# Keys and queries of a linear-attention block, computed for paired token tiles as seven block products instead of eight

## The chip, the cores and the metric

The kernel runs on one core of one Trainium2 chip. The metric is device time in microseconds (us) of one execution. Runs of the kernel before took 1123.71, 1124.23 and 1126.42 us; their median, 1124.23, is the time to compare with.

A core has a matrix engine, TensorE (PE in the profile; PEld is its weight load), a vector engine, VectorE (DVE), ScalarE (ACT), GpSimd (POOL), and a queue on SyncE (SP) that issues all transfers (DMAs) here. They share an on-chip memory (SBUF); TensorE writes to a small accumulator memory (PSUM) of eight banks, which the other engines empty.

## The reference

For 2,048 tokens of 576 features in fp32:

```python
xn = layernorm(x)
q, k, v = split(xn @ wqkv)              # 32 heads of 18
phi = lambda t: where(t > 0, t + 1, exp(t)) + 1e-6
kv = einsum("hsd,hse->hde", phi(k), v); z = phi(k).sum(over tokens)
s = (phi(q) @ kv) / (phi(q) . z + 1e-6) @ wo
g = silu(gelu(xn @ w1 + b1) @ w2 + b2)  # 4608 hidden
out = x + s * g
```

## The kernel before, in words

**Arithmetic.** TensorE multiplies in a rounded fp32 format (fp32r). So each fp32 operand is split into a high part (a cast, on ACT) and a low part (operand minus high part, on DVE or POOL), and a product of 128 rows of the contraction takes three matmuls: high x high, high x low, low x high. The 576 features are four blocks of 128 and a rest of 64, whose high and low parts lie in one tile of 128 rows. So the projection of one token tile of 128 to 576 columns is 14 steps, each in two halves of 288 columns: 28 matmuls of 128x288 (`project`, L219).

**Stage 1 (0 to 153 us).** For each of 16 token tiles: layernorm statistics (`layernorm`, DVE L168 to L180, a power on POOL L173), the normalized tile xn (ACT, L191), five transposes on TensorE (L196), the split of the transposed tile (ACT L204, DVE L205 and L206), K and V projections (L219), phi of K (L226 to L229), and the state kv, a sum over tokens kept in two banks (`state`, L256). Beside this the 27 sums of blocks of w2 that the last stage needs are made: subtraction on POOL (L288), cast on ACT (L296), low part on DVE (L301), a store. The weights are split at the start (`split_w`, L243 and L244).

**Stage 2 (153 to 298 us).** kv is folded with wo into one matrix (`fold_wo`, L518 to L525, right after the first two queries). For each tile: Q projection (`query`, L219), phi, the denominators (POOL L546, DVE L550 to L554, POOL L555), five transposes (`transpose_p`, L574), and 28 matmuls with the folded matrix (`attend`, L592). Beside this, `XSums` makes sums and differences of blocks of x (L337 to L341) in long operations for each half of the tokens.

**Stage 3 (298 to 1122 us).** The two layers of the feed-forward part, for two halves of 1,024 tokens in nine chunks of hidden features each. Each layer multiplies 2 x 2 blocks with seven block products instead of eight (a Strassen scheme with operands summed ahead): `Up` (L819, moving operand 128x512) and the products of the second layer (L950). At the half switch x's operands of the second half are loaded from device memory (`load_x_part`, L1115, seven DMAs of 8.1 MB together); the last chunk of the second half is done in plain products (`down_plain`, L1074 and L1087).

**What sets the order.** In stages 1 and 2 every instruction stands in its engine's queue in the order of the program text (`in_order`): an instruction that waits holds up all behind it on its engine. All DMAs stand in one queue. PSUM has three tiles of two banks, used in turn for transposes, K, V, Q and `attend`, and two single banks, for the state and for `fold_wo`.

## Time and profile before

| what | before |
|---|---|
| median of three runs | 1124.23 us |
| span of the profiled execution | 1122.4 us |
| mean granted TensorE clock | 0.995 of full speed |
| PE busy, share of the span | 1108.1 us, 99% |
| DVE / ACT / POOL busy | 811.9 / 456.8 / 443.0 us |
| moved by DMA | 246.7 MB, mean 220 GB/s |

The profile is of one execution; its span runs from the first to the last instruction, and the time of an execution is about 1.8 us above it. A window row gives, for a stretch of time, each engine's busy time with its number of instructions, the granted TensorE clock, the share of time that the DMA engines were busy, and GB/s. A timeline row gives start and duration of neighbouring like instructions, and in brackets the idle time of the engine before them and what ended it. A row of instruction groups gives the line, the engine, the operation, output<-inputs, shapes, the count, then busy time, the mean of one in ns, and the idle time before.

### The profile page before, as it was taken

What the parts mean: (1) busy time and instruction counts of PE and PEld (TensorE: products, weight loads), DVE (VectorE), ACT (ScalarE), POOL (GpSimd) and SP (SyncE); (2) the same over time, 40 slices, a digit from 0 to 9 for tenths busy, and PEclk for the clock granted to TensorE, in tenths of its full rate; (3) what the DMA queues carried; (4) which work ended last, traced back from release to release, by engine and by line L of the source; (5) the groups of instructions that cost most, each with busy time, mean ns of one, the idle gap of its engine ahead of it and who ended that gap; (6) DMA issues with size and microseconds to landing.
All of it is one profiled execution on the core that took longest, in us unless ns stands there. A gap on an engine that the chain in (4) does not pass through costs nothing.

```text
span 1122.4 us, 18619 instructions
## 1 busy us (share of the span) xinstructions
PE 1108.1 (99%) x7008; PEld 1026.8 (91%) x7008; DVE 811.9 (72%) x1185; ACT 456.8 (41%) x801; POOL 443.0 (39%) x368
## 2 busy tenths in 40 slices
...
GB/s 295 193 335 301 222 124 41 33 172 160 228 224 342 170 241 301 160 290 206 205 340 172 262 244 389 368 254 258 221 208 212 214 204 211 231 197 222 84 170 88
DMA packets 83367, 246.71 MB, mean 220 GB/s; under 512 B 9229, under 2 KB 19981, under 8 KB 79695
## 3 DMA queue, kind: packets, MB, share of 16 engines
...
q8 instruction: 55, 0.90, 0.3%
...
## 4 chain that ended last, share of the span: by engine, by line
PE 95%; DVE 3%; DMA 0%; POOL 0%; ACT 0%; issue 0%; SPq 0%; DVEq 0%; ACTq 0%; POOLq 0%
PE pm L950 34%; PE e L819 12%; PE a L819 10%; PE zy L819 10%; PE pv L219 5%; PE pk L219 5%; PE b L819 4%; PE ps_s L592 4%; PE pq L219 4%; PE pd L1074 2%; PE ps_kva L256 1%; PE pt L196 1%; DVE xt L337 1%; PE ps_kw L518 1%; PE ptp L574 0%; DMA w<-wqkv 0%
## 5 line engine op out<-in xcount | busy, mean ns | idle before, releaser
L957 DVE TENSOR_TENSOR macc<-pm,macc 128x576 f32<-128x576 f32 x218 | 164.2, 753 | 56.9 <-PE pm L950 56.3
L616 ACT CAST h_h<-g 128x512 fp32r<-128x512 f32 x204 | 120.9, 621 | 139.8 <-PE pm L950 138.7
L619 DVE TENSOR_TENSOR h_l<-g,h_h 128x512 fp32r<-128x512 f32 x204 | 172.3, 844 | 0.0
L918 POOL TENSOR_TENSOR mid<-g 128x512 f32<-128x512 f32 x34 | 44.1, 1296 | 187.7 <-ACT g L827 187.7
L827 ACT ACTIVATE g<-b,b1c 128x512 f32<-128x512 f32 x36 | 24.8, 688 | 121.8 <-DVE b L845 121.7
L836 ACT COPY mid<-a 128x512 f32<-128x512 f32 x36 | 21.1, 585 | 109.3 <-PE a L819 109.3
L819 PE MATMUL a<-h0r,wa 128*128 128x512 f32 x180 | 58.6, 390 | 0.0
L819 PE MATMUL a<-xh,wa 128*128 128x512 f32 x180 | 58.5, 390 | 0.0
L839 DVE TENSOR_TENSOR mid<-b,mid 128x512 f32<-128x512 f32 x36 | 24.8, 689 | 46.5 <-PE b L819 35.4
L915 POOL TENSOR_TENSOR g<-g 128x512 f32<-128x512 f32 x34 | 52.4, 1542 | 13.1 <-DVE h_l L619 11.8
L912 POOL TENSOR_TENSOR g<-g 128x512 f32<-128x512 f32 x34 | 49.5, 1456 | 17.9 <-DVE h_l L619 16.6
L1044 POOL TENSOR_TENSOR fin1l<-fin1h,fin1l 128x288 f32<-128x288 f32 x8 | 6.4, 805 | 121.4 <-DMA fin1l<-s_dram 45.1
L819 PE MATMUL zy<-xh,w 128*128 128x512 f32 x144 | 50.2, 389 | 0.0
L819 PE MATMUL zy<-h1r,w 128*128 128x512 f32 x144 | 50.2, 389 | 0.0
L641 POOL TENSOR_TENSOR w1t<-w1raw 128x256 f32<-128x256 f32 x18 | 17.6, 977 | 81.4 <-DVE w L619 81.4
L909 POOL TENSOR_TENSOR g<-g 128x512 f32<-128x512 f32 x34 | 47.7, 1402 | 2.7
L852 DVE TENSOR_TENSOR e<-e,mid 128x512 f32<-128x512 f32 x36 | 25.1, 697 | 27.1 <-PE e L819 27.0
L555 POOL TENSOR_TENSOR pbuf<-phiq,den 128x576 f32<-128x576 f32 x16 | 20.9, 1305 | 57.8 <-DVE den L554 52.9
L827 ACT ACTIVATE g<-e,b1c 128x512 f32<-128x512 f32 x36 | 24.8, 689 | 43.0 <-DVE e L852 43.0
L288 POOL TENSOR_TENSOR w2r<-w2r 128x576 f32<-128x576 f32 x27 | 41.1, 1528 | 0.7
L819 PEld LDWEIGHTS a<-xh,wa 128*128 128x128 f32 x180 | 33.8, 188 | 6.8
L819 PEld LDWEIGHTS a<-h0r,wa 128*128 128x128 f32 x180 | 33.8, 188 | 6.8
...
## 6 DMA issues: line engine op xcount, KB each, us to landing
...
```

The lines of the kernel that those rows point to most:

```text
L219: nc.tensor.matmul(ps[:, h, :HD], st, w[:, k, h * HD : (h + 1) * HD], start=(i == 0), stop=(i == len(seq) - 1),)
L592: nc.tensor.matmul(ps[:, h, :HD], st[:, k, :], w[:, k, h * HD : (h + 1) * HD], start=(i == 0), stop=(i == len(seq) - 1),)
L616: nc.scalar.copy(pair[0], src)
L619: eng.tensor_tensor(pair[1], src, pair[0].bitcast(F32), op=SUB)
L819: nc.tensor.matmul(ps, st, mv, start=first and n == 0, stop=n == len(seq) - 1, skip_group_check=True,)
L827: nc.scalar.activation(g, ps, AF.Gelu_apprx_tanh, bias=b1c[:, f : f + 1])
L909: tt(src[5, pr], A(1, 0), A(1, 1), op=ADD)
L912: tt(src[6, pr], src[5, pr], A(0, 0), op=SUB)
L915: tt(src[3, pr], A(0, 1), src[6, pr], op=SUB)
L918: tt(src[7, pr], A(0, 0), A(1, 0), op=SUB)
L950: nc.tensor.matmul(ps[:, q, :HD], hs[p][st][:, cs], m[:, p, :], start=(n == 0 and i not in CHAIN), stop=(n == len(seq) - 1), skip_group_ch ...
L957: nc.vector.tensor_tensor(dst, src, dst, op=ADD)
```

## The change

**Pairs and seven products.** The 16 token tiles form eight pairs: pair p has the tiles t and t + 4, of the first eight tiles for p below 4 in the order of `pair_tile`, else of the last eight. For a pair, the projection to K is a product of 2 x 2 blocks (two tiles by two halves of the columns, and two halves of the features), and the class `Proj` makes it from seven block products A, B, Z, E (four one-bank tiles, each used up to twice): 50 matmuls of 128x288 instead of 56. The rest of 64 features is added in three of the products. This is done for K in pairs 2 to 7 and for Q in all eight; K of pairs 0 and 1, and V, stay plain (`Plain`). Drains are now separate operations of 288 columns: u1, u2 and the sums on DVE, the rest on ACT.

**Operands.** The weights' sums for the seven products are made by POOL (`sums`, four subtractions of 128x576), and split by ACT and DVE, for K in pair 1 and for Q at the end of stage 1. The sums of x (`x_sum`, `s_hi`, `s_lo`) are made in stage 1, pair by pair, and kept for stages 2 and 3; `XSums` is gone. x lies in four tiles xH, xL, xSH, xSL with 128 columns of one pair together, so the moving operand of `Up` is four runs of 128 columns instead of one of 512. Every pair's x is stored to device memory (`x_store`); the queries of the second half's pairs come first (`Q_ORDER`), the first half's x is loaded back pair by pair in stage 2 (`x_reload`), and at the half switch four DMAs of whole tiles load the second half's (`x_swap`).

**PSUM.** Stages 1 and 2 have four single banks (psA), one two-bank tile for transposes (psT) and two single banks for the state, later for `attend` (psS). The pools of before are opened for stage 3.

**Order.** Stage 1 has a hand-written opening for pair 0 and a table of steps (14 for each pair) for the rest; so has stage 2. The denominators of a pair are made one pair later, `attend` two pairs later, in parts between the queries' other work. Of the w2 sums 9 stay in stage 1 and 18 move to stage 2. `fold_wo` comes after the first pair of queries, uses the four banks, and its drains alternate between ACT and DVE. In layernorm, a 128x1 operation of DVE (L180) becomes a DVE scaling and a POOL multiplication; phi is now exp on ACT, one DVE operation on SBUF data (`phi_max`) and an addition on ACT.

Three places where instructions move. First ACT, from the last weight cast of K on. In the names, wv_h is V's high part, raw_ its source, pt_ a transposed x tile, pk_/pl_ and pv_ the products' banks. Before:

```order
L243 CAST wk_h<-w_4_154 128x576
L243 CAST wv_h<-raw_v 128x576 x4
L243 CAST wv_h<-raw_v_143 128x576
L204 CAST xh_86<-pt_246 128x5x128
L226 ACTIVATE ek_264<-pk_207 128x576
L434 COPY v_298<-pv_269 128x576
```

After, where k_162 is K of the first tile, drained in two halves, and v_158 its V:

```order
L413 ACTIVATE k_162<-pl_230,c_84 128x288
L413 ACTIVATE k_162<-pl_231,c_84 128x288
L431 CAST wv_h<-raw_207 128x576 x2
L280 CAST xH<-pt_262 128x384
L281 CAST x_tmp0h<-pt_262 128x256
L431 CAST wv_h<-raw_207 128x576 x2
L431 CAST wv_h<-rr_208 128x576
L411 COPY v_158<-pl_283 128x288
L411 COPY v_158<-pl_284 128x288
```

The casts of V's weights stood ahead of all work on the first K; now its drains, which wait for that projection, stand ahead of them.

Second DVE, around the statistics of a tile (BN_STATS, BN_AGGR; x_ is the raw tile). Before, in the third round of stage 1 (ek_ and phik_ belong to phi):

```order
L205 TENSOR_TENSOR xl_87<-pt_339,xh_86 128x4x128
L206 TENSOR_TENSOR xh_86<-pt_339,xh_86 64x128
L168 BN_STATS st_348<-x_205 128x6
L169 BN_STATS st_348<-x_205 128x6
L171 BN_AGGR mv_351<-st_348 128x2
L172 TENSOR_SCALAR mv_351<-mv_351 128x1
L180 SCALAR_TENSOR_TENSOR mv_351<-mv_351 128x1
L227 TENSOR_SCALAR ek_357<-ek_357 128x576
L229 SCALAR_TENSOR_TENSOR phik_360<-pk_310,ek_357 128x576
```

After, at the end of pair 0; scr holds the sums of x, k_163 is K of the pair's second tile, st_441 belongs to the first tile of pair 2:

```order
L290 TENSOR_TENSOR xL<-pt_366,xH 128x512
L294 TENSOR_TENSOR xH<-pt_366,xH 64x128
L317 TENSOR_TENSOR xSL<-scr,xSH 128x1024
L321 TENSOR_TENSOR xSH<-scr,xSH 64x128
L438 SCALAR_TENSOR_TENSOR k_163<-e_161,k_163 128x576
L240 BN_STATS st_441<-x_393 128x6
L241 BN_STATS st_441<-x_393 128x6
L243 BN_AGGR mv_444<-st_441 128x2
L244 TENSOR_SCALAR mv_444<-mv_444 128x1
L247 TENSOR_SCALAR mv_444<-mv_444 128x1
```

The low part of the sums and phi now stand ahead of the statistics.

Third, DVE in pair 1: the rows that read pt_584, the transposes of pair 2's second tile, and what stands ahead of them (wt_521 and wt_522 are the sums of K's weights that POOL makes):

```order
L438 SCALAR_TENSOR_TENSOR k_164<-e_160,k_164 128x576
L157 TENSOR_TENSOR wkq_l<-wt_521,wkq_h 128x1152
L292 TENSOR_TENSOR xL<-pt_584,xH 128x256
L294 TENSOR_TENSOR xH<-pt_584,xH 64x128
L310 TENSOR_TENSOR scr<-scr,pt_584 128x256
L310 TENSOR_TENSOR scr<-pt_584,scr 128x256
L310 TENSOR_TENSOR scr<-scr,pt_584 128x128
L298 TENSOR_TENSOR x_tmp0l<-pt_584,x_tmp0h 128x256
L157 TENSOR_TENSOR wkq_l<-wt_522,wkq_h 128x1152
```

Before, the tile of the transposes was read by L204 to L206 alone, and no weight sums were made; now the low part of these sums stands ahead of all readers on DVE, and the next transposes use the same PSUM tile.

The diff, cut to its core:

```diff
-    psum = ctx.enter_context(tc.tile_pool(name="psum", bufs=3, space=PSUM))
-    psum1 = ctx.enter_context(tc.tile_pool(name="psum1", bufs=2, space=PSUM))
+    pse = ExitStack()
+    psA, psT, psS = (
+        pse.enter_context(tc.tile_pool(name=n, bufs=b, space=PSUM, reuse_waits="tile"))
+        for n, b in (("psA", 4), ("psT", 1), ("psS", 2))
+    )
     dram = ctx.enter_context(tc.tile_pool(name="dram", bufs=1, space=bass.MemoryType.DRAM))
...
+    x_tiles = [
+        xp.tile([P, 4, n, P], F32R, tag=v, name=v)
+        for v, n in (("xH", 8), ("xL", 6), ("xSH", 9), ("xSL", 8))
+    ]
+    xH, xL, xSH, xSL = (t.rearrange("p c k j -> p k c j") for t in x_tiles)
+    X_PARTS = ((xH, 0, 8), (xL, 8, 14), (xSH, 14, 23), (xSL, 23, 31))
+    scr = xp.tile([P, 2560], F32, tag="mid", name="scr")
+
...
-    x_dram = dram.tile([P, 31, 512], F32, name="x_dram")
...
+    x_dram = [dram.tile([P, 4, 31, P], F32, name=f"x_dram{i}") for i in range(2)]
...
+    def pair_tile(p, s):
+        return 8 * (p < NPAIR // 2) + p % 4 + 4 * s
...
+        def sums(self, raw, eng):
...
+            for i, u, v in ((5, f1a, f0a), (6, f1b, T[5]), (7, f1b, f1a), (4, f0b, T[6])):
+                eng.tensor_tensor(T[i], u, v, op=SUB)
+
+        def split_sums(self, j, elo):
+            self.put(lambda t: t[:, 3 + 2 * j : 5 + 2 * j], self.t[j], elo)
...
+        if not first:
+            nc.vector.tensor_scalar(mv[:, 0:1], mv[:, 0:1], -1.0, None, op0=MUL)
+            nc.gpsimd.tensor_tensor(mv[:, 2:3], mv[:, 0:1], mv[:, 3:4], op=MUL)
...
+        pt = psT.tile([P, 1024], F32, tag="pt", name=f"pt{p}{s}")
...
+    def x_sum(p, i, eng, b=None):
+        a, b = xf(p, 0), pts[p, 1] if b is None else b
+        s1, s2, s3, s4 = (s_raw[:, k : k + 2] for k in (0, 2, 4, 6))
+        out, u, v, op = {
+            1: (s1, s2, a[:, 0:2], ADD), 3: (s3, a[:, 0:2], b[:, 0:2], SUB),
+            2: (s2, b[:, 2:4], s3, SUB), 4: (s4, a[:, 2:4], s2, SUB),
+            5: (s_raw[:, 8], a[:, 4], b[:, 4], SUB),
+        }[i]
+        eng.tensor_tensor(out, u, v, op=op)
+
+    def s_hi(p):
+        nc.scalar.copy(xSH[:, :, pair_cols(p)], s_raw)
+
+    def s_lo(p):
...
+    def x_store(p):
+        cs = pair_cols(p)
+        for t, a, b in X_PARTS:
+            nc.sync.dma_start(x_dram[p // 4][:, cs, a:b], t[:, :, cs].bitcast(F32))
+
+    def x_reload(i):
+        cs = pair_cols(Q_ORDER[4 + i // 4])
+        t, a, b = X_PARTS[(1, 2, 3, 0)[i % 4]]
+        nc.sync.dma_start(t[:, :, cs].bitcast(F32), x_dram[0][:, cs, a:b])
...
+    class Proj:
...
+            self.A, self.B, self.Z, self.E = (bank(f"{v}{p}")[:, :HD] for v in "abze")
...
+        def step(self, i):
+            A, B, Z, E = self.A, self.B, self.Z, self.E
+            tt = nc.vector.tensor_tensor
+            add1 = lambda out, ps, u: nc.vector.scalar_tensor_tensor(out, ps, 1.0, u, op0=ADD, op1=ADD)
+            a, b = self.dst
+            if i == 1:
+                self.mm(A, 1)
+                nc.scalar.copy(self.m1, A)
+            elif i == 6:
+                self.mm(B, 6)
+                tt(self.u1, B, self.m1, op=ADD)
+            elif i == 7:
+                self.mm(Z, 7)
+                tt(self.u2, Z, self.u1, op=ADD)
+            elif i == 5:
+                self.mm(E, 5, (1, 1))
+                add1(b[:, HD:], E, self.u2)
+            elif i == 2:
+                self.mm(A, 2, (0, 0), first=False)
+                nc.scalar.activation(a[:, :HD], A, AF.Identity, bias=one)
+            elif i == 3:
+                self.mm(E, 3, (1, 2), first=False)
+                add1(a[:, HD:], E, self.u1)
+            else:
+                self.mm(Z, 4, (0, 1))
+                add1(b[:, :HD], Z, self.u2)
...
+            if b == n_all:
+                for n in range(2):
+                    d = self.dst[:, n * HD : (n + 1) * HD]
+                    if self.bias is None:
+                        nc.scalar.copy(d, self.ps[n])
+                    else:
+                        nc.scalar.activation(d, self.ps[n], AF.Identity, bias=self.bias)
...
+    def phi_exp(r, e):
+        nc.scalar.activation(e, r, AF.Exp, bias=minus_one)
+
+    def phi_max(r, e):
+        nc.vector.scalar_tensor_tensor(r, e, 1.0, r, op0=ALU.min, op1=ALU.max)
+
+    def phi_add(r):
+        nc.scalar.activation(r, r, AF.Identity, bias=tiny)
...
+    plain_k(0, 0).part(0, N14)
+    transpose_x(0, 1)
+    split_v(0, kt_raw(raw_v, 0), DV)
+    split_v(1, kt_raw(raw_v, 1), GP)
+    x_hi(0, 1), x_lo_tmp(0), x_lo(0, 1)
+    split_v(2, kt_raw(raw_v, 2), DV)
+    split_v(3, kt_raw(raw_v, 3), GP)
+    split_v(4, rest_v, DV)
+    plain_v(0, 0).part(0, N14)
+    x_stats(1, 0)
+    x_raw(0, 1)
+    for i in (3, 2, 1, 5, 4):
+        x_sum(0, i, GP, xf(0, 1))
+    k_t = k_ts[0]
+    phi_exp(k_t[0], e_t[0])
+    x_norm(1, 0)
+    plain_k(0, 1).part(0, N14)
+    transpose_x(1, 0)
+    phi_max(k_t[0], e_t[0]), phi_add(k_t[0])
+    x_stats(1, 1)
+    x_hi(1, 0), x_lo(1, 0)
+    x_raw(1, 0)
+    x_norm(1, 1)
+    s_hi(0), s_lo(0)
+    load_x(2, 0)
+    load_x(2, 1)
+    x_store(0)
+    plain_v(0, 1).part(0, N14)
+    phi_exp(k_t[1], e_t[1]), phi_max(k_t[1], e_t[1])
+    transpose_x(1, 1)
+    x_stats(2, 0)
+    x_hi(1, 1), x_lo_tmp(1), x_lo(1, 1)
+    phi_add(k_t[1])
+    x_norm(2, 0)
+    load_x(3, 0)
+    load_x(3, 1)
+    w2_load(0, w2p, "w2r")
+
+    def do_state(p):
+        for s in range(2):
+            state(2 * p + s, k_ts[p % 2][s], v_t[s])
...
+        add(base + 3, do_state, p - 1)
+        if p == 1:
+            sums(1, (0, 0, 0, 1, 1), 2, 3, GP)
+            for s in range(2):
+                add(base + 8, k_sum, k_ts[0][s])
+            add(base + 1, x_stats, 2, 1)
+            add(base + 3, x_norm, 2, 1)
+            add(base + 2, transpose_x, 2, 0)
+            add(base + 2, x_hi, 2, 0)
+            add(base + 3, x_raw, 2, 0)
+            add(base + 3, x_lo, 2, 0)
+            add(base + 5, transpose_x, 2, 1)
+            add(base + 5, x_hi, 2, 1)
+            add(base + 6, x_lo, 2, 1)
+            sums(2, (6, 6, 6, 6, 7), 8, 9, GP)
+            add(base + 6, x_lo_tmp, 2)
+            add(base + 7, wkq.split_sums, 1, DV)
+            prepare(3, 0, 4, 6, 10, 11)
+            prepare(3, 1, 7, 12, None, None)
+            add(base + 2, wkq.sums, raw_k, GP)
+            add(base, load_x, 4, 0)
+            add(base + 6, load_x, 4, 1)
+            add(base + 5, wkq.split_sums, 0, DV)
+        else:
+            if p + 2 < NPAIR:
+                prepare(p + 2, 0, 0, 5, 10, 11)
+                prepare(p + 2, 1, 7, 11, None, None)
...
+    for p in range(1, NPAIR):
+        plan_pair(p)
+        base = p * NSP
+        if p > 1:
+            pr = Proj(p, wkq, k_ts[p % 2], mu1)
+            steps = [(pr.step, (i,)) for i in K_UP]
...
+        for k, (fn, args) in enumerate(steps):
+            fn(*args)
+            at_step(base + k)
+        for s in range(2):
+            pr = plain_v(p, s)
+            for k, v in enumerate(((0, 5), (5, 10), (10, 14))):
+                pr.part(*v)
+                at_step(base + 7 + 4 * s + k)
+            if s == 0:
+                at_step(base + 10)
...
-                ps = bank1(f"ps_kw{i}{n}{h}")[:n, :HD]
+                ps = bank(f"ps_kw{i}{n}{h}")[:n, :HD]
...
+                    (nc.vector.tensor_copy if h else nc.scalar.copy)(kw[i][:n, hs], ps)
...
+    RELOAD = {0: (0, 1), 1: (2, 3, 4), 2: (5, 6, 7), 3: (8, 9, 10), 4: (11, 12, 13), 5: (14, 15)}
+    for r in range(NPAIR + 2):
+        base = (NPAIR + r) * NSP
+        if r <= 5:
+            for k, i in enumerate(RELOAD[r]):
+                add(base + (9, 11, 12)[k], x_reload, i)
+        if r < NPAIR:
+            a, b = q_tiles(r)
+        if 2 <= r <= NPAIR:
+            add(base, den_mul, r - 1, 1)
+            add(base + 2, den_sum, r - 1, 0)
+            add(base + 2, den_div, r - 1, 0)
+            add(base + 3, den_sum, r - 1, 1)
+            add(base + 3, den_div, r - 1, 1)
+        if 1 <= r < NPAIR:
...
+            pr = Proj(Q_ORDER[r], wkq, q_tiles(r), mu2)
+            for k, i in enumerate(K_UP):
+                pr.step(i)
+                if (r, k) == (2, 0):
+                    transpose_p(0, 1)
+                if (r, k) == (1, 5):
+                    transpose_p(0, 0), p_hi(0, 0), p_lo(0, 0)
+                at_step(base + k)
...
-                    ps, st, mv, start=first and n == 0, stop=n == len(seq) - 1,
+                    ps.rearrange("p (c j) -> p c j", c=4), st, mv, start=first and n == 0, stop=n == len(seq) - 1,
...
-    def load_x_part(k):
-        a, b, make_tile, at = X_PARTS[k]
-        x_new[k] = make_tile(at, f"{k}r")
-        nc.sync.dma_start(x_new[k].bitcast(F32), x_dram[:, a:b])
+    def x_swap(k):
+        _, a, b = X_PARTS[k]
+        nc.sync.dma_start(x_tiles[k].bitcast(F32), x_dram[1][:, :, a:b])
...
-                for k, at in {"h0": 13, "l0": 13, "s2": 13, "h1": 15, "l1": 15, "s1": 15, "s4": 15}.items():
-                    add(base + at, load_x_part, k)
+                for k, at in ((0, 13), (1, 13), (2, 15), (3, 15)):
+                    add(base + at, x_swap, k)
```

905 lines of the change are left out of this document (483 added, 422 removed), and 4 rows, old and new, of the table SUMS.

## The prediction

> **What bounds the kernel now.** I read the page first: the busy shares, then the chain that ended last.
>
> ```profile
> PE 1108.1 (99%) x7008; PEld 1026.8 (91%) x7008; DVE 811.9 (72%) x1185; ACT 456.8 (41%) x801; POOL 443.0 (39%) x368
> PE 95%; DVE 3%; DMA 0%; POOL 0%; ACT 0%; issue 0%; SPq 0%; DVEq 0%; ACTq 0%; POOLq 0%
> ```
>
> TensorE (PE) is busy all the time and is 95% of the chain, so removed matmuls are worth their full pace, and every wait put on PE costs in full. The stretches of the two stages that change, read by windows, and then one by one the microseconds around the only hole:
>
> ```profile
> core 0: us, PE busy (x) PEld busy (x) DVE busy (x) ACT busy (x) POOL busy (x), PEclk, DMA share, GB/s
> 15.00:30.00 15.00, 14.92 (x116) 14.71 (x115) 9.76 (x21) 4.82 (x8) 7.24 (x7) 1.00 0.54 218
> 60.00:75.00 15.00, 15.00 (x118) 15.00 (x117) 11.04 (x21) 6.73 (x12) 8.10 (x7) 1.00 1.02 420
> 180.00:195.00 15.00, 11.28 (x56) 10.35 (x56) 14.56 (x20) 3.52 (x7) 5.75 (x4) 0.68 0.02 8
> ...
> 185.00:186.00 1.00, 1.00 (x8) 1.00 (x7) 1.00 (x1) 0.00 (x0) 0.00 (x0) 0.67 0.08 16
> 186.00:187.00 1.00, 1.00 (x6) 1.00 (x5) 0.96 (x2) 0.00 (x0) 0.00 (x0) 0.50 0.00 0
> ...
> 194.00:195.00 1.00, 1.00 (x6) 1.00 (x6) 1.00 (x2) 0.00 (x0) 0.00 (x0) 0.50 0.28 106
> 195.00:196.00 1.00, 1.00 (x8) 1.00 (x7) 0.90 (x3) 0.00 (x0) 0.00 (x0) 0.71 0.50 189
> ```
>
> Stage 1 has no hole after its start. At the change to stage 2, VectorE (DVE) is full, PE loses 3.7 of 15 us, and the granted clock is 0.50 for nine to ten microseconds. The timeline there gives the holes, and the pace of matmuls:
>
> ```profile
> 180.87 0.43 PE L219 MATMUL pq<-wq_h,xl 128*128 128x288 f32 x2
> 181.40 0.43 PE L219 MATMUL pq<-wq_l,xh 128*128 128x288 f32 x2
> 183.52 0.74 PE L574 MATMUL ptp<-ident,pbuf 128*128 128x128 f32 x5 [1.69 <-DVE phiq L229]
> 184.43 0.51 PE L592 MATMUL ps_s<-kw_h,th 128*128 128x288 f32 x2 [0.17 <-DVE th L580]
> 189.23 0.85 PE L592 MATMUL ps_s<-kw_l,th 128*128 128x288 f32 x2 [1.86 <-DVE kw_l L244]
> ```
>
> **The change part by part.** Term 1, the products: 14 pairs go from 56 to 50 matmuls of 128x288, 84 fewer. From the start 180.87 to 181.40 four matmuls pass, 0.1325 us each: 84 x 0.1325 = **-11.1 us** (4.8 in stage 1, 6.4 in stage 2). A tile's projection is 28 x 0.1325 = 3.7 us.
>
> What this costs is on the other engines, in the order of their rows. The durations I use (behind the count: busy us, mean ns of one, then the engine's idle us before them and what ended it):
>
> ```profile
> L288 POOL TENSOR_TENSOR w2r<-w2r 128x576 f32<-128x576 f32 x27 | 41.1, 1528 | 0.7
> L173 POOL TENSOR_TENSOR mv<-mv,nhalf 128x1 f32<-128x1 f32 x16 | 8.8, 550 | 59.3 <-DVE mv L172 59.3
> L641 POOL TENSOR_TENSOR w1t<-w1raw 128x256 f32<-128x256 f32 x3 | 3.4, 1117 | 1.3 <-DVE w L619 1.3
> L244 POOL TENSOR_TENSOR wk_l<-w,wk_h 128x576 fp32r<-128x576 f32 x3 | 5.5, 1842 | 0.6 <-ACT wk_h L243 0.6
> L243 ACT CAST wv_h<-raw_v 128x576 fp32r<-128x576 f32 x5 | 3.4, 674 | 1.1 <-DMA raw_v<-wqkv 0.8
> L191 ACT ACTIVATE xn<-x,mv 128x576 f32<-128x576 f32 x14 | 12.2, 872 | 13.9 <-DVE mv L180 13.9
> L191 ACT ACTIVATE xn<-x,mv 128x64 f32<-128x64 f32 x14 | 6.0, 425 | 0.0
> L204 ACT CAST xh<-pt 128x640 fp32r<-128x640 f32 x15 | 10.4, 692 | 19.8 <-PE pt L196 19.8
> L340 ACT CAST s<-xt 128x1024 fp32r<-128x1024 f32 x3 | 3.2, 1050 | 0.0
> L522 ACT COPY kw<-ps_kw 126x288 f32<-126x288 f32 x8 | 3.2, 398 | 1.4 <-PE ps_kw L518 1.2
> L518 PEld LDWEIGHTS ps_kw<-wo,kvz 126*126 126x126 f32 x16 | 2.5, 186 | 2.1 <-ACT kw L522 1.9
> L168 DVE BATCH_NORM_STATS2 st<-x 128x6 f32<-128x288 f32 x16 | 7.3, 454 | 3.7 <-DMA x<-x 3.6
> L171 DVE BATCH_NORM_AGGREGATE mv<-st 128x2 f32<-128x12 f32 x16 | 3.3, 209 | 0.5
> L172 DVE TENSOR_SCALAR mv<-mv 128x1 f32<-128x1 f32 x16 | 2.5, 154 | 0.6
> L341 DVE TENSOR_TENSOR s<-xt,s 128x1024 fp32r<-128x1024 f32 x3 | 4.3, 1426 | 1.1 <-ACT s L340 1.0
> L229 DVE SCALAR_TENSOR_TENSOR phik<-pk,ek 128x576 f32<-128x576 f32 x16 | 12.1, 758 | 0.6
> ```
>
> Term 2, the first V projection. Before:
>
> ```profile
> 12.85 0.77 PE L196 MATMUL pt<-ident,xn 128*128 128x128 f32 x5 [0.61 <-DVE xn L177]
> 13.37 0.51 PE L219 MATMUL pv<-wv_h,xh 128*128 128x288 f32 x2
> 12.94 3.42 DVE L244 TENSOR_TENSOR wv_l<-raw_v,wv_h 128x576 fp32r<-128x576 f32 x5
> 17.50 0.64 ACT L434 COPY v<-pv 128x576 f32<-128x576 f32 x1 [2.60 <-PE pv L219]
> ```
>
> Five transposes take 0.52 us from start to start. V's low parts are done at 16.36, the projection about 17.4 (its drain starts at 17.50). After the change, ScalarE (ACT) does two drains of K first, which wait for K's end (12.85 - 0.61 = 12.2), then two casts, two of x, then three casts: the fourth starts near 15.9 and ends near 16.6. Its low part is now GpSimd's (POOL): 1.84 us, 18.4. Six matmuls are left behind it: 19.2. **+1.8**, between 0 (POOL's at DVE's 3.42/5 = 0.68) and 3.
>
> Term 3, the second pair's transposes. From 19.2 PE runs K, transposes, V, transposes, K: 31.4 us, and then wants the normalized tile (2,0). That comes out of a chain over four engines: two V drains and a copy (20.7); POOL's five sums of pair 0, four at 1.05 (the 1.12 of 128x256, a little less while DVE has no long work) and one at 0.55 (25.4); POOL's pow and multiply for tile (1,1), 2 x 0.55 (26.5); xn on ACT, 1.2 (27.7); the cast of the sums, 1.15 (28.9); DVE's low part 1.43 + 0.3 (30.6) and phi_max 0.76 (31.4); only then the statistics of tile (2,0), 0.45 + 0.45 + 0.21 + 2 x 0.15 (32.8), POOL 1.1 (33.9), xn (34.7 to 35.1). **+3.3**, and +0.5 for the transposes of (1,1), which wait for 27.7 instead of 27.2. Bounds: 1 (the copies shorter) to 5. Before, the statistics of a tile stood ahead of phi on DVE.
>
> Term 4, the third pair's. PE goes on from 35.4 with two states (each 10 matmuls at the 0.1 of a transposing one, 2.0), K 3.7, transposes, V 3.7 and is at the transposes of (3,0) near 45.7. They need the single two-bank tile that (2,1) still holds. It is read by DVE rows that stand behind the low part of K's weight sums. POOL begins these four sums after (2,1)'s multiply, near 37.3: 4 x 1.53 = 43.4; cast of 128x1152, 1.15 (44.6); low part, 1.43 x 1152/1024 = 1.6 (46.2); then six short DVE operations on the tile, about 2.2 (48.4). **+2.7**, bounds 0.5 to 4.5.
>
> Term 5, the drains. A pair's product Z takes the bank of V's second tile, which ACT empties behind x's two copies (0.69 each by the size of the 640-wide cast), xn (1.3) and phi. Between V's end and Z lie 14 matmuls, 1.86 us; ACT needs 2.1 to 3.2. So 0.4 to 1.3 in each of four or five pairs, **+3.5**, and 2.0 in pair 2, where the queue is longest: **+2.0**. Bounds for both 1 to 9. With the added sums DVE has about 13.9 of 17.1 us to do per pair and ACT 12.5, which hides the rest; if that cover fails, K's pairs run at DVE's pace.
>
> Term 6, the clock. By the shares 0.67 and 0.71 of the windows above, 0.50 lasted from 185.3 to 195.6, 10.2 us, after holes of 1.69 and 0.17 us within four. I take one such spell in stage 1, since terms 3 and 4 are longer holes: half of what PE worked in it, (10.2 - 1.86)/2 = **+4.2**. Bounds 0 and two spells, 8.4.
>
> The Trainium skill ("TensorE: Matmul & The Clock Gate", Part 1: The HAM clock gate) has the half clock come after a whole idle window of about 3.4 us. The trace has it after less idle time, 1.69 us in a thinly filled stretch; by the page's rule term 6 would be 0 and the sum 1124, near (b) below.
>
> Term 7, the change of stage. Now 1.69 + 0.17 + 1.86 + 4.2 = 7.9 us are lost, and 1.9 more in the fold of wo, whose weight loads wait for drains (row of L518). After: the denominators lie a pair later and the fold has four banks, but Q's second and third pair wait for banks and for single drains, by the same durations 1.05 + 0.55 + 1.35 + 0.85 + 0.95 + 0.6 = 5.3, spread over 30 us. 9.8 - 5.3: **-4.5**, bounds -9.8 and 0. The later pairs of stage 2 have 15.1 us of PE beside 10.4 of DVE, 9.1 of ACT and 10.1 of POOL, and cost nothing.
>
> Term 8, the half switch at 684 us. Seven reloads become four, x's low and high first. The transfers before and after fill the queues:
>
> ```profile
> 684.00:686.00 2.00, 2.00 (x16) 1.92 (x15) 1.50 (x3) 1.48 (x3) 0.00 (x0) 1.00 1.00 424
> 706.00:708.00 2.00, 2.00 (x13) 1.78 (x12) 1.88 (x4) 0.00 (x0) 1.82 (x1) 1.00 0.97 400
> 706.74 0.40 PE L819 MATMUL a<-h0r,wa 128*128 128x512 f32 x1
> 706.98 0.40 PE L819 MATMUL a<-l0r,wa 128*128 128x512 f32 x1
> ```
>
> 8.1 MB of x and 1.3 MB of weights at 0.41 MB/us take 22.9 us; Up wants the first part 22.4 us after its end and the last some microseconds later. **+1**, bounds 0 and 4. x's extra stores and w2's later operands go over queues with room (share 0.54 in the window from 15 us) or that were full without a hole on PE (1.02 from 60 us): nothing.
>
> Sum: -11.1 + 1.8 + 3.8 + 2.7 + 5.5 + 4.2 - 4.5 + 1 = +3.4 on the profiled span of 1122.4; the median of the runs, 1124.23, lies 1.8 above that span, so 1127.6, given as **1128 us**. A change under 0.3%, 3.4 us, can't be told from none here: same is 1120.9 to 1127.6.
>
> **The rivals.** (a) Faster, 0.34: the queues of terms 3 to 5 dissolve, since ACT's and POOL's short operations overlap more than their sums say, and the clock stays whole. For: PE had no hole in stage 1 with DVE at 11 of 15 us. Against: the order of rows is fixed on each engine. It decides where terms 3 to 6 together stay under 7 us instead of 16.2. At 4 us, with 2 us less loss at the change of stage: 1124.2 - 11.1 + 1.8 + 4 - 6.5 + 1 = 1113.
>
> (b) No half clock, 0.1: the holes as summed, but each long one has full work on both sides, where the one of 1.69 us had a second hole and single waits behind it: 1127.6 - 4.2 = 1123.4.
>
> (c) The x tiles are now four runs of 128 columns each, so Up's moving operand is not one run. No row has such an operand; Up has 50 matmuls in each of 36 blocks, 1,800, so each nanosecond more costs 1.8 us. Lower bound 0; upper bound far: as four transposes of 128 columns (0.52/5 each) it is 0.42 instead of the 0.24 between the starts 706.74 and 706.98. I take 0, the nearest row, that of the same 512 columns. At 10 ns: 1146, chance 0.04.
>
> (d) The swap's last part, now one whole tile, is late by 4 us and brings another spell of half clock: 1128 + 3 + 4 = 1135, chance 0.07.
>
> (e) DVE operations with two SBUF operands stretch beside POOL. The row of the V weights had 3.42/5 = 0.68 for one, with POOL idle behind its first part; the same shape beside POOL:
>
> ```profile
> L244 DVE TENSOR_TENSOR wq_l<-w,wq_h 128x576 fp32r<-128x576 f32 x2 | 2.4, 1259 | 0.4 <-ACT wq_h L243 0.4
> ```
>
> So up to 0.6 us more for an operation. phi_max read PSUM and now reads SBUF twice; with the sums' low parts five or six of these stand in the chains of terms 3 to 5: 1128 + 3 = 1131, chance 0.08. The Trainium skill ("SBUF — State Buffer", SBUF: two separate sides) calls the pair of ports that the two share an exclusive lock; the rows agree in kind.
>
> **How the numbers follow.** My forecast has 0.37; of it a third falls within 0.3%. Faster: (a) 0.34 and a little of (b) and the forecast's lower edge, 0.38. Same: 0.12 of the forecast and most of (b), 0.18. Slower: 0.44. The range reaches from (a), 1113 less 3, to (d) and (e) with 3 more: 1110 to 1138; the forecast's own is 1123 to 1134.
>
> **What would show it.** Right: PE with 84 matmuls fewer; holes of 2 to 4 us near 31 and 46 us, released by xn and by DVE; a granted clock of 0.50 somewhere before 60 us; no hole over 1.5 us between 150 and 200. Wrong: PE full from 20 us on (a), Up's matmuls more than 0.24 us apart (c), or a hole behind 706 us that ends with a transfer (d).

## The result and the profile after

The changed kernel took 1142.35 us in the median (1141.04 to 1145.28), the kernel before 1124.29 in the same session: a ratio of 1.0156, 95% interval 1.0133 to 1.0179. It is slower by 18 us, outside the predicted range; the forecast of 1128 had the sign and not the size.

The page of the profiled execution of the changed kernel, its busy line and its chain:

```profile
PE 1108.3 (97%) x6924; PEld 1020.3 (89%) x6924; DVE 827.6 (72%) x1250; ACT 503.4 (44%) x913; POOL 473.8 (41%) x403
PE 78%; DVE 7%; ACT 6%; DMA 5%; issue 2%; POOL 1%; SPq 0%; DVEq 0%; ACTq 0%; POOLq 0%
```

84 matmuls, 11.1 us of products, are gone, and PE is as long busy as before. In part this is half clock: behind the holes below it lasted 17.1 us in all, before the change 10.2. The rest was not separated; the first product behind a wait is busy 0.40 us, where its neighbours take 0.29 or 0.30. The chain has fallen from 95% to 78% PE; DVE, ACT and transfers now end waits. The span is 1143.6 us against 1122.4 (this execution, 1145.28, is the highest of its four, 3 us above their median).

Where the 21.2 us of the span went can be read from the starts of the stages in the timeline of PE. The first rows of Q and of `Up` before, then those of Q, of the fold, of the next Q product and of `Up` after the change:

```profile
152.84 0.43 PE L219 MATMUL pq<-wq_h,xh 128*128 128x288 f32 x2
...
298.05 0.39 PE L819 MATMUL a<-xh,wa 128*128 128x512 f32 x1
```

```profile
162.45 0.40 PE L349 MATMUL a<-wkq_h,xH 128*128 128x288 f32 x1 [0.86 <-ACT v L411]
...
172.41 6.48 PE L789 MATMUL ps_kw<-wo,scr 126*126 126x288 f32 x24
178.52 0.51 PE L349 MATMUL a<-wkq_h,xH 128*128 128x288 f32 x1
...
310.69 0.39 PE L1123 MATMUL a<-xH,wa 128*128 128x512 f32 x1
```

So stage 1 is 9.6 longer, stage 2 (Q to `Up`) 3.0, and stage 3 8.6. One tile's state, about 1 us of PE, has moved over the first of these borders: one state stands behind the first Q row before, two after. With the same work on both sides stage 1 is 10.6 longer and stage 2 only 2.0. Predicted were 13.2, -10.9 and +1.

**Stage 1.** The holes on PE, in the timeline:

```profile
35.06 0.77 PE L270 MATMUL pt<-ident,xn 128*128 128x128 f32 x5 [2.83 <-DVE scr L310]
48.53 0.74 PE L270 MATMUL pt<-ident,xn 128*128 128x128 f32 x5 [1.06 <-ACT wkq_h L156]
55.85 0.40 PE L349 MATMUL z<-wkq_h,xSH 128*128 128x288 f32 x1 [1.02 <-ACT v L411]
74.38 0.40 PE L349 MATMUL z<-wkq_h,xSH 128*128 128x288 f32 x1 [0.99 <-ACT v L411]
```

They stand where terms 3, 4 and 5 put them; the row of Z comes again in pairs 4 to 6. At the first hole the normalized tile was done at 34.85, and DVE's last reader of the transposes' tile, which the row names, at 34.92; both stand behind the same statistics on DVE. At the second DVE's last reader of that tile ends at 48.39; the cast that the row names ends at the same moment and does not touch the tile. Behind the first one the clock falls, in windows of 2 us:

```profile
36.00:38.00 2.00, 2.00 (x11) 2.00 (x10) 0.72 (x3) 1.69 (x3) 1.92 (x4) 0.50 1.10 369
38.00:40.00 2.00, 2.00 (x16) 2.00 (x16) 1.99 (x2) 2.00 (x5) 1.92 (x2) 0.74 0.95 252
```

**Change of stage.** PE, and ACT that it waits for:

```profile
185.09 0.40 PE L349 MATMUL a<-wkq_h,xH 128*128 128x288 f32 x1 [2.75 <-ACT scr L361]
192.28 0.34 PE L840 MATMUL ptp<-ident,pbuf 128*128 128x128 f32 x1 [2.76 <-ACT pbuf L832]
201.27 0.40 PE L349 MATMUL z<-wkq_h,xH 128*128 128x288 f32 x1 [0.80 <-DVE scr L367]
203.20 0.40 PE L349 MATMUL e<-wkq_h,xSH 128*128 128x288 f32 x1 [0.60 <-DVE rt L357]
```

```profile
184.06 0.67 ACT L774 CAST kw_h<-kr 128x576 fp32r<-128x576 f32 x1 [4.15 <-DMA kr<-kw]
184.64 0.39 ACT L361 COPY scr<-a 128x288 f32<-128x288 f32 x1
191.02 0.67 ACT L774 CAST kw_h<-kr 128x576 fp32r<-128x576 f32 x1 [5.99 <-DMA kr<-kw]
191.60 0.49 ACT L373 ACTIVATE scr<-a,c 128x288 f32<-128x288 f32 x1
192.00 0.23 ACT L832 COPY pbuf<-pbuf 128x64 f32<-128x64 f32 x1
```

The releaser that PE names, a drain of 0.39, is not the cause. ACT stood idle for 4.15 and 5.99 us in front of a cast of a folded row (kr), whose transfer had not landed, and A's drain stands behind that cast in ACT's order. Before, the same casts had no wait:

```profile
174.64 0.68 ACT L243 CAST kw_h<-kr 128x576 fp32r<-128x576 f32 x1
182.38 1.24 ACT L243 CAST kw_h<-kr 128x576 fp32r<-128x576 f32 x2
```

They stood 5.4 and 13.1 us behind the end of the fold (169.24); now ACT comes to the first two 1.4 and 6.5 us behind it (178.52).

In the chain of waits between 170 and 200 us the transfer is the longest piece:

```profile
179.27 11.68 DMA kr<-kw
```

The two holes have half clock behind them:

```profile
187.00:189.00 2.00, 2.00 (x10) 1.98 (x10) 0.05 (x1) 0.00 (x0) 0.00 (x0) 0.50 0.67 182
194.00:196.00 2.00, 2.00 (x10) 1.98 (x10) 1.58 (x4) 0.31 (x2) 0.00 (x0) 0.50 0.97 406
```

The later Q pairs follow each other at 16.19 us (Z at 217.86, 234.05, 250.23) instead of the 15.1 of the prediction:

```profile
234.05 0.40 PE L349 MATMUL z<-wkq_h,xH 128*128 128x288 f32 x1 [0.24 <-DVE scr L367]
235.62 0.40 PE L349 MATMUL e<-wkq_h,xSH 128*128 128x288 f32 x1 [0.25 <-DVE rt L357]
```

Each wait of 0.24 costs 0.41 from start to start beyond the pace of 0.13.

**Half switch.** PE, and windows with the clock:

```profile
725.86 0.80 PE L1123 MATMUL b<-xSL,w 128*128 128x512 f32 x1 [4.36 <-DMA xSL<-x_dram]
```

```profile
726.00:732.00 6.00, 6.00 (x15) 4.66 (x16) 2.05 (x3) 2.12 (x2) 0.00 (x0) 0.50 1.04 406
```

The transfers run full (1.04) and the last tile, xSL, comes 4.36 us late; then 6 us at 0.50. The chain of waits ahead of it (SPq is the queue that issues the transfers, L1396 those of x):

```profile
697.49 3.20 PE pm L1254 x24
...
700.71 0.33 SPq L1193
...
701.09 0.54 SPq L1396
...
701.68 24.14 DMA xSL<-x_dram
```

The last product that reads xSL starts at 694.59, and `Up` ends at 697.3. But xSH and xSL are issued at 701.09 and 701.68, since a load of the second layer's operand (L1193) stands ahead of them in the queue and waits until 700.69 for products. From the second half's first `Up` to the end it is 423.9 us after and 415.7 before.

### The profile page after: what moved, and what is told of

It reads as the page before. It is cut to its first block, busy times and chain, and to the rows that moved or that the text cites. A ratio compares the mean times of both kernels' runs of the same rounds, so it can differ in the third digit from the quotient of the medians.

```text
span 1143.6 us, 18714 instructions
## 1 busy us (share of the span) xinstructions
PE 1108.3 (97%) x6924; PEld 1020.3 (89%) x6924; DVE 827.6 (72%) x1250; ACT 503.4 (44%) x913; POOL 473.8 (41%) x403
## 4 chain that ended last, share of the span: by engine, by line
PE 78%; DVE 7%; ACT 6%; DMA 5%; issue 2%; POOL 1%; SPq 0%; DVEq 0%; ACTq 0%; POOLq 0%
PE pm L1254 32%; PE e L1123 12%; PE zy L1123 10%; PE a L1123 10%; PE b L1123 4%; DMA xSL<-x_dram 2%; PE pl L404 2%; PE pd L1371 2%; DVE w2o L509 2%; PE ps_s L872 1%; PE ps_kva L457 1%; PE e L349 1%; PE z L349 1%; DVE k L438 1%; DMA kr<-kw 1%
## 5 line engine op out<-in xcount | busy, mean ns | idle before, releaser
L1123 PE MATMUL a<-xH,wa 128*128 128x512 f32 x360 | 117.1, 390 | 0.0
L1123 PEld LDWEIGHTS a<-xH,wa 128*128 128x128 f32 x360 | 67.6, 188 | 13.7
L1123 PE MATMUL e<-xSH,wb 128*128 128x512 f32 x216 | 67.8, 395 | 0.2 <-DVE b L1149 0.2
L1219 POOL TENSOR_TENSOR g<-g 128x512 f32<-128x512 f32 x34 | 52.5, 1544 | 13.1 <-DVE h_l L902 11.8
L1123 PE MATMUL a<-xL,wa 128*128 128x512 f32 x144 | 56.2, 390 | 0.0
L1123 PEld LDWEIGHTS e<-xSH,wb 128*128 128x128 f32 x216 | 40.5, 188 | 12.7 <-DVE b L1149 4.5
L1123 PE MATMUL zy<-xSH,w 128*128 128x512 f32 x144 | 51.1, 396 | 0.0
L1123 PE MATMUL b<-xSH,w 128*128 128x512 f32 x144 | 50.9, 394 | 0.0
L1123 PE MATMUL e<-xSH,w 128*128 128x512 f32 x144 | 50.6, 392 | 0.0
L1123 PE MATMUL zy<-xH,w 128*128 128x512 f32 x144 | 50.2, 389 | 0.0
```

The costliest lines, as they stand in the source:

```text
L1123: nc.tensor.matmul(ps.rearrange("p (c j) -> p c j", c=4), st, mv, start=first and n == 0, stop=n == len(seq) - 1, skip_group_check=True,)
L1219: tt(src[3, pr], A(0, 1), src[6, pr], op=SUB)
```

## The experiments

Each is compared with the changed kernel's 1142.35 and, by its ratio, with the kernel before. The changed kernel's four runs lie 4.2 us apart, so a difference of one to three us says little by itself; what counts there is which waits the trace shows gone.

**1. The swap in blocks.** x of the second half comes in blocks for each product, each right after its last use, instead of four whole tiles after all.

```diff
-                for k, at in ((0, 13), (1, 13), (2, 15), (3, 15)):
-                    add(base + at, x_swap, k)
+                for k, i in enumerate(UP):
+                    add(base + 7 + k, x_swap, i)
```

> The changed kernel, with the reload of x at the half switch cut into the seven product blocks of Up and issued in the order in which the last Up of the first half has done with them, instead of four whole tiles. Theory A (the whole tiles can't start before the last product of the first half has read them, and the second product of the second half needs the tile that comes last): the hole of 4.4 us at 725 us and the spell of half clock behind it go, 1142.4 becomes 1134 to 1136. Theory B (the queues are full anyway, the bytes decide): the hole stays within 1 us of 4.4 and the time within 2 us of 1142.

1137.09 us, ratio 1.0115 [1.0099, 1.0131]: 5.3 less. In the same window the clock is whole and no wait for a transfer is left:

```profile
726.00:732.00 6.00, 6.00 (x29) 4.95 (x28) 1.92 (x3) 3.35 (x5) 0.00 (x0) 1.00 1.03 403
```

From the second half's start to the end it is now 415.5 us, as before the change. So the whole loss of stage 3 comes from x's late transfers, 8.2 in the profiled execution and 5.3 in the medians. The run changes the pieces and their places in the queue at once (the first is issued at 687.22, ahead of the load that waits), and does not part the two.

**2. The folded rows' casts later.** All three are moved from the first two Q pairs into the third.

```diff
-        if r == 1:
-            add(base + 3, split_kw, 2, nc.vector)
-            add(base + 5, split_kw, 3, nc.vector)
+        if r == 2:
+            for k in (1, 2, 3):
+                add(base + 3 + k, split_kw, k, nc.vector)
...
-            split_kw(1, nc.vector)
```

> The changed kernel, with the casts and low parts of the three row blocks of the folded matrix that come by DMA moved behind the drains of the third pair of queries (second round of stage 2), instead of ahead of the second pair's drains. Theory A (ACT stands still in front of these casts until the DMAs of the folded rows land, 4.2 and 6.0 us, and the queries' drains behind them hold up PE): both holes of 2.8 us near 185 and 192 us and the half clock go, 1142.4 becomes 1133 to 1137. Theory B (the denominators or the transposes behind them are late as well): the holes only move, less than 2 us.

1140.89, 1.0148 [1.013, 1.0165]: 1.5 less. The holes of 2.75 went, and one of 2.35 came, with two smaller ones behind it:

```profile
204.49 0.53 PE L872 MATMUL ps_s<-kw_h,th 128*128 128x288 f32 x2 [2.35 <-ACT kw_h L774]
```

```profile
203.62 0.24 ACT L832 COPY pbuf<-pbuf 128x64 f32<-128x64 f32 x1 [5.44 <-POOL pbuf L823]
203.77 1.24 ACT L774 CAST kw_h<-kr 128x576 fp32r<-128x576 f32 x2
```

ACT now waited for POOL in front of a small copy, and the casts, ready by then, stood behind that. Theory B, for another queue than I named.

**3. The same casts by another place.** The first two at steps 9 and 12 of the second pair, the last at step 1 of the third.

```diff
+        if r in (1, 2):
+            for k, at in {1: ((1, 9), (2, 12)), 2: ((3, 1),)}[r]:
+                add(base + at, split_kw, k, nc.vector)
```

> The changed kernel again with the three casts of the folded rows moved, but to other places than before: two to the end of the second pair's round, one to the second step of the third, each behind drains that PE waits for and ahead of the two copies that wait for POOL. Theory A (what counts is that no drain stands behind a wait for the folded rows, and no cast of them behind a wait for POOL): PE's holes between 178 and 215 us fall from about 9 to 4 us and the time from 1142.4 to 1135 to 1138. Theory B (the rows land too late wherever the casts stand, or the denominators are late): 1140 or more.

1140.08, 1.0137 [1.0121, 1.0152]: 2.3 less. The hole went to Z (3.14 at 198.72, released by DVE), since two low parts on DVE took 2.75 us together beside POOL's denominators, where one takes 0.75 alone:

```profile
193.36 2.75 DVE L775 TENSOR_TENSOR kw_l<-kr,kw_h 128x576 fp32r<-128x576 f32 x2 [1.41 <-ACT kw_h L774]
```

**4. Cast and low part apart.** On top of experiment 6 below: the first row's cast at the end of the second pair's products, the other two at steps 1 and 3 of the third pair, ahead of the pads, and their low parts at 5 and 6.

```diff
+        if r == 2:
+            for k, hi, lo in ((2, 1, 5), (3, 3, 6)):
+                add(base + hi, kw_hi, k)
+                add(base + lo, kw_lo, k, nc.vector)
```

> The changed kernel with the low part of the attention tile later (e_plo) and the folded rows' casts one by one: the first at the end of the second pair's products, the other two before the copies that wait for POOL, their low parts on DVE after the sums of Q. Theory A (the loss at the change of stage is one of order, in which each of these operations held up a drain or a sum behind it): PE's holes from 178 to 215 us fall from 9 to under 3.5 us, with no half clock there, and 1139.2 (e_plo) becomes 1133 to 1136. Theory B (it only moves again, as in the first two tries): 1137 or more.

1136.39, 1.0107 [1.0092, 1.0123]: 2.8 less than experiment 6 alone, between the two theories. No half clock is left there. It is the best of the three places, though Z still waits 1.24, and a transpose 1.14.

**5. The reloads of x one pair later.** Is it their traffic that makes the folded rows late?

```diff
-    RELOAD = {0: (0, 1), 1: (2, 3, 4), 2: (5, 6, 7), 3: (8, 9, 10), 4: (11, 12, 13), 5: (14, 15)}
+    RELOAD = {1: (0, 1, 2), 2: (3, 4, 5), 3: (6, 7, 8), 4: (9, 10, 11), 5: (12, 13, 14), 6: (15,)}
```

> The changed kernel, with the sixteen reloads of x in stage 2 spread one round later, so that none is issued while the folded matrix is moved between rows. Theory A (the reloads share the queues with these row transfers and delay them to 11.7 us): the cast that waited 6.0 us waits 2 to 3 us less, 1142.4 becomes 1138 to 1140. Theory B (the row transfers take as long by themselves): the same holes, 1141 to 1144.

1141.08, 1.0145 [1.0128, 1.0163]: 1.3 less, not beyond the scatter of the two. The first cast waits as long as it did, the second 1.1 less:

```profile
184.38 0.67 ACT L774 CAST kw_h<-kr 128x576 fp32r<-128x576 f32 x1 [4.14 <-DMA kr<-kw]
190.25 0.67 ACT L774 CAST kw_h<-kr 128x576 fp32r<-128x576 f32 x1 [4.90 <-DMA kr<-kw]
```

So the row transfers take most of that time by themselves. While the second cast waits, the DMA engines are hardly busy (0.11, the worth of two of the 16):

```profile
186.00:191.00 5.00, 3.81 (x18) 3.52 (x16) 1.22 (x4) 0.75 (x2) 0.00 (x0) 0.66 0.11 41
```

With transfers that slow, what was wrong is that ACT asks for the rows so early.

**6. The low part p_lo three steps later.** In each Q pair it stood on DVE between the two drains u1 and u2.

```diff
-            add(base + NSP + 1, p_lo, r - 1, 1)
+            add(base + NSP + (4 if r < NPAIR - 1 else 1), p_lo, r - 1, 1)
```

> The changed kernel, with the low part of the transposed attention tile (0.97 us of DVE) moved from between the sums u1 and u2 of a pair of queries to three steps later. Theory A (u2 comes late, so the bank Z isn't free for its second product): the two waits of 0.4 us with their slow restarts go in five or six pairs, 1142.4 becomes 1137 to 1139. Theory B (the operands of w2, stretched to 1.8 us by POOL beside them, hold up u1, and that alone is enough): the waits stay at over half, 1140 to 1142.

1139.18, 1.013 [1.0115, 1.0145]: 3.2 less. The waits at Z are gone and a pair takes 15.66 us; those at E (0.20 to 0.30), behind a denominator's sum on DVE, stay:

```profile
233.72 0.40 PE L349 MATMUL e<-wkq_h,xSH 128*128 128x288 f32 x1 [0.21 <-DVE rt L357]
```

**7. xn of a pair's second tile three steps earlier.** It stood on ACT ahead of V's drain.

```diff
-                prepare(p + 2, 1, 7, 11, None, None)
+                prepare(p + 2, 1, 7, 8, None, None)
```

> The changed kernel, with the normalization of a pair's second tile on ACT moved in pairs 2 to 5 from ahead of the last V drains into the gap in which ACT waits for phi. Theory A (V's drains are late because xn's 1.2 us stand ahead of them): the holes of 1.0 us before Z go in pairs 3 to 6, 1142.4 becomes 1137 to 1139. Theory B (phi's DVE operation, stretched to 1.4 us beside POOL, sets ACT's pace): 0.5 us or less each, 1140 to 1142.

1138.5, 1.0119 [1.0102, 1.0136]: 3.9 less. The group of Z's first matmul between 50 and 140 us, in the changed kernel and here, with PE's idle time ahead of it at the end:

```profile
L349 PE MATMUL z<-wkq_h,xSH 128*128 128x288 f32 x10 | 3.5, 348 | 5.0 <-ACT v L411 5.0
```

```profile
L349 PE MATMUL z<-wkq_h,xSH 128*128 128x288 f32 x10 | 3.5, 348 | 1.0 <-ACT v L411 1.0
```

Only pair 2, which the edit leaves as it was, still waits.

**8. Without the sums of K over the tokens in pairs 2 to 7.** POOL's long additions are left out, so most tokens are missing in the denominators; DVE's operations that stood beside them then run alone.

```diff
-            add(base + 8, k_sum, ka)
...
-        add(base + 10, k_sum, kb)
```

> The changed kernel without POOL's sums of K over the tokens in pairs 2 to 7 (the denominators then lack most tokens; left out only to free POOL). Theory A (DVE's phi and low parts take 1.4 instead of 0.75 and 0.3 us while POOL sums, and by that V's drains are late): DVE's rows go back to 0.75 and 0.3, the 1.0 us holes before Z shrink to under 0.5 and the time falls by 2 to 4 us. Theory B (ACT's own queue sets it): holes as before, within 1 us.

1139.87, 1.0139 [1.0124, 1.0154]: 2.5 less. The waits at Z fall from 5.0 to 2.7:

```profile
L349 PE MATMUL z<-wkq_h,xSH 128*128 128x288 f32 x10 | 3.5, 348 | 2.7 <-ACT v L411 2.7
```

So about half of these waits comes from POOL's additions, through DVE held up beside them or through the powers of the statistics that stand behind them in POOL's queue; the run does not part the two. That DVE is held up is seen directly. The last operation of s_lo, 64x128, in its eight pairs (minimum, median and maximum in ns), in the changed kernel and here:

```profile
L321 DVE TENSOR_TENSOR xSH<-scr,xSH x8: 290/1412/1553, 30.4 to 145.7; 64x128 fp32r<-64x128 f32 x8
```

```profile
L321 DVE TENSOR_TENSOR xSH<-scr,xSH x8: 289/290/1553, 30.5 to 142.8; 64x128 fp32r<-64x128 f32 x8
```

In the changed kernel it takes 0.29 us in pair 0, with POOL idle, and 1.41 in pair 1, beside POOL's weight sums.

**9. The opening in another order.** V's casts ahead of K's drains and all low parts on DVE; the statistics of tile (2,0) ahead of the sums; phi of the second tile in pair 1.

```diff
+    for k in range(4):
+        split_v(k, kt_raw(raw_v, k), DV)
+    split_v(4, rest_v, DV)
     plain_k(0, 0).part(0, N14)
...
-    split_v(1, kt_raw(raw_v, 1), GP)
...
-    s_hi(0), s_lo(0)
...
+    x_stats(2, 0)
+    s_hi(0), s_lo(0)
```

> The changed kernel with another opening: V's weights are cast ahead of the first K's drains, all their low parts on DVE; the statistics of tile (2,0) stand ahead of the low part of pair 0's sums, phi of the pair's second K behind the readers of the transposed tile. Theory A (terms 2 and 3 as predicted are queues of order): the holes of 2.3 us in the first V and of 3.0 us near 32 us go, and the half clock behind the latter too, 1142.4 becomes 1134 to 1138. Theory B (the transposed tile of pair 0 and the four-engine chain are late anyway): 1139 to 1142.

1140.31, 1.0143 [1.0126, 1.016]: 2.0 less. The holes in the first V are gone and the one of 2.83 is 1.09, but the transposes of (2,1) now wait, and have half clock behind them:

```profile
39.51 0.79 PE L270 MATMUL pt<-ident,xn 128*128 128x128 f32 x5 [1.95 <-DVE xH L294]
```

**10. All together.** Experiments 1, 4 (with 6), 7 (pair 1 too) and 9, and the weights' sums a few steps earlier on POOL.

```diff
+    wkq.sums(raw_k, GP)
...
-            add(base + 2, wkq.sums, raw_k, GP)
...
-            prepare(3, 1, 7, 12, None, None)
+            prepare(3, 1, 7, 9, None, None)
```

> All repairs together in the changed kernel: the reload at the half switch in product blocks (singly worth 5.3 us), the low part of the attention tile later (3.2), xn of the second tile earlier, now in pair 1 as well (3.9), the casts and low parts of the folded rows at places where neither a drain nor a sum of Q stands behind them (up to 5), the opening (2.0) with POOL's weight sums made 12 us earlier, which should take the hole of 2.0 us ahead of the third pair's transposes and its half clock. If the singly measured parts add up: 1142.4 - 5.3 - 3.2 - 3.9 - 4 - 4 = 1122, between 1118 and 1126. If they overlap, because one late engine hides behind the other: 1127 to 1132. Against the kernel before, only a part of the 11.1 us of matmuls saved would then be kept.

1123.8 (1123.47 to 1126.75), ratio 1.0008 [0.9999, 1.0017]: 18.5 less than the changed kernel, and the same as before. PE's busy time shows the saved products at last (1100.3 for 1108.3):

```profile
PE 1100.3 (98%) x6924; PEld 1015.5 (91%) x6924; DVE 826.2 (74%) x1252; ACT 502.9 (45%) x913; POOL 471.9 (42%) x401
```

The parts, measured one by one, add up to 5.3 + 6.0 (3.2 and 2.8) + 3.9 + 2.0 = 17.2. That is in part chance: the transposes of (2,0) wait 2.55 us here, where experiment 9 had 1.09.

**11. Twelve moves more.** In the opening the sums of x earlier on POOL, in pair 1 statistics and weight splits earlier, in stage 2 denominators later.

```diff
+    x_raw(0, 1)
+    for i in (3, 2, 1):
+        x_sum(0, i, GP, xf(0, 1))
     plain_v(0, 0).part(0, N14)
...
-            add(base + 2, den_sum, r - 1, 0)
+            add(base + 3, den_sum, r - 1, 0)
...
+            add(base + 3, den_all, 0, 1)
```

> The kernel with all parts (e_all) still shows holes on TensorE that have a releaser each: 2.55 at the transposes (2,0) behind the low part of the first pair's sums (and half clock after it), 1.05 at (3,0) behind the low part of the weights' sums, 1.00 at Z of pair 2 behind V's drain, 0.85 before the first Q product behind the last V drains, 1.24 at Z of the second Q pair behind both denominators on DVE, 0.44 and 0.83 in the third, 2.26 at a transpose behind a sum of w2 on POOL and the pads on ACT, and five waits of 0.24 to 0.29 (with their restart 0.4) at E behind a denominator's sum on DVE. This kernel reorders the program text at each of these places (twelve small moves; nothing is left out of the computation). Theory A, each hole is the price of one instruction that stands ahead of a drain, and goes when that is moved: about 10 holes worth 9 to 10 us together, and a half-clock spell of 1 to 2: 1111 to 1116, faster than both kernels. Theory B, the engines beside TensorE are full there and the holes come back one place later, as they did for the casts of the folded rows: 1119 to 1124.

1127.13, 1.0028 [1.0017, 1.0039]: 3.3 more than experiment 10. At the change of stage the holes of 1.24 and 0.44 went; new ones opened in stage 1 (1.61 at 23.00, behind xn; 2.53 at 41.66, behind a low part that waits for POOL), and in four Q pairs the later denominators made a transpose wait:

```profile
41.66 0.74 PE L270 MATMUL pt<-ident,xn 128*128 128x128 f32 x5 [2.53 <-DVE xH L294]
...
234.13 0.74 PE L846 MATMUL ptp<-ident,pbuf 128*128 128x128 f32 x5 [0.53 <-DVE th L858]
```

**12. The good half of them.** Experiment 10 with the moves at the change of stage, and the low part of the weights' first sums one step earlier.

```diff
-            for s in range(2):
-                den_all(0, s)
+            den_all(0, 0)
...
+        if r == 1:
+            add(base + 3, den_all, 0, 1)
...
+            for k, hi, lo in ((2, 1, 3), (3, 1, 4)):
```

> The twelve moves of the run before (e_best) fell in two parts: in stage 1 they opened new holes (1.6 at the transposes (1,0), 2.5 at (2,1), 1.7 before A of pair 2), and the later denominators of the Q pairs made a transpose wait 0.5 in four pairs; between the fold's end and the second Q pair's end they took out the holes at Z (1.24) and at A (0.44). This kernel is the one with all parts (e_all, 1123.8) with the good half alone: the second denominator of the first Q pair one pair later, phi's addition and its product behind the next product's drain, the sums of w2 behind the division in the third Q pair, the low parts of the last two folded rows three steps earlier, and the low part of the weights' first two sums one step earlier in pair 1. Theory A, these holes have their own instructions and do not depend on the rest: 1.0 (transposes (3,0)), 1.7 (Z, A), 0.8 (kw_l) and 2.3 to 2.7 (the transpose of the third pair): 5.8 to 6.2 less, 1116 to 1119. Theory B, what is won at the change is lost again before stage 3, since DVE is busy there without a break: 1121 to 1124.

1123.24, 0.9991 [0.9982, 1.0]: theory B. From the fold's end to stage 3 it is 1.9 us shorter (123.3 for 125.2), and stage 1 1.1 longer, since A of pair 2 now waits 1.34 behind V's drain. What was won at Z came back as a wait for a low part on DVE:

```profile
193.49 0.85 PE L876 MATMUL ps_s<-kw_l,th 128*128 128x288 f32 x2 [2.27 <-DVE kw_l L776]
```

No version tried is measurably faster than the kernel before.

## Why the prediction was wrong, and where right

**Term 1** held: 84 matmuls fewer. The step that failed most is **term 7** with its clause that the later pairs of stage 2 "cost nothing". With the same work on both sides stage 2 is 2.0 longer although 6.4 of products went: +8.4 instead of -4.5, a miss of 12.9. The holes and the half clock of the old change of stage (7.9) did go, but two things came in their place. The casts of folded rows that wait for transfers were not in my list of waits at all (I summed drains of 0.55 to 1.35): the two holes of 2.75 and 2.76, 5.5 us, and 6.8 us of half clock behind them, some 3.4 more. So the sign "no hole over 1.5 us between 150 and 200" failed. Experiments 2 to 4 confirm the cause by moving it, 5 shows that the reloads have little part in it. And the later pairs take 16.19 instead of 15.1, some 1.1 in each of five or six. I had compared sums of engine time (10.4 of DVE in 15.1), which say nothing of a drain that stands behind the wrong operation: 0.97 of p_lo between u1 and u2 was enough for half of it (experiment 6).

**Term 8**, the half switch, was mis-sized: +1 with bounds to 4, measured +8.6 in the profile and 5.3 in the medians (experiment 1). The arithmetic of 22.9 us of transfers against 22.4 of cover took them to start at the end of `Up` and to run without a break. Two of the four tiles were issued 4 us after that end, behind a load that waits, and the last of them landed at 725.8, 28.5 us after it; what else than the late issue made it 28.5 was not separated. Then the hole brought half clock. That is rival (d) as a mechanism, priced at 7 and given 0.07.

**Terms 2 to 6** came to 18.0 in the sum and about 15.4 in the trace (10.6 and the 4.8 of products), each at its place: the K behind the first V starts 1.7 later than before (1.8), the transposes of (2,0) with those of (1,1) wait 3.5 from start to start (3.8), (3,0) 1.2 (2.7), Z 5.0, or 6.3 with the slower restarts (5.5). Term 6's spell of half clock came where it was put, behind (2,0), but for 3.4 us and not 10.2, a cost of 1.7 and not 4.2. Term 4 is small for a reason that the sum did not have: the tile came free at 48.39, as forecast (48.4), but PE, slowed by that spell, wanted it at 47.3 and not at 45.7. One hole was not foreseen, 0.86 ahead of the first Q product.

**Rivals.** (a) fell: the queues did not dissolve. (b) fell: the clock was 0.50 in four stretches. They stood behind holes of 2.83, 2.75, 2.76 and 4.36 us; experiment 9 has one behind 1.95. By the rule of the Trainium skill ("TensorE: Matmul & The Clock Gate", Part 1: The HAM clock gate) that a whole idle window of about 3.4 us must pass, only the hole at the half switch is long enough for one. The trace differs in the other three, and the measurement decides. (c) fell: the groups of `Up`'s products by form, before and after, with minimum, median and maximum in ns, are the same to the nanosecond:

```profile
L819 PE MATMUL a<-xh,wa x180: 387/389/398, 298.1 to 680.2; 128*128 128x512 f32 x180
```

```profile
L1123 PE MATMUL a<-xH,wa x360: 387/389/398, 310.7 to 1106.9; 128*128 128x512 f32 x180
```

(e) is right in kind: a median of 0.29 against 1.41 us in experiment 8, which puts some 2.5 us of the whole on K's sums alone, by this or by POOL's own queue. The Trainium skill ("SBUF — State Buffer", SBUF: two separate sides) has a DVE operation with two SBUF inputs and a GpSimd operation that reads SBUF exclude each other at a shared pair of ports. The rows agree in kind.

## What to carry to other kernels

When a change cuts the work of the bounding engine, walk each other engine's order and ask of every drain what stands ahead of it, and of that, what it waits for: a cast that waits for a transfer holds up every drain behind it (PE lost 2.75 of the 4.15 us and 2.76 of the 5.99), whatever the drain's own 0.4 us. Sums of engine time show room on average and miss this. Walk the queue of transfers in the same way: a load that waits holds up the loads behind it. A load that takes the place of data still in use should come in the pieces in which that data is given up, each as soon as it is (experiment 1 has the two together).

## What the runs showed beyond that

A transfer of folded rows from one place in on-chip memory to another stands in the chain of waits with 11.7 us, against 0.67 for the cast that needs it, and the first cast's wait hardly changed (4.15 to 4.14) with the reloads out of the way. The DMA engines were then 0.11 busy at 41 GB/s, so it was not a full queue that the second cast waited for. Why these transfers keep so few engines busy, no run shows.

Half clock came in steps of 3.4 us, worked out from the shares of windows of 1 us as in term 6: 3.4 behind the hole at 35.06, 3.4 behind each of those at 185.09 and 192.28, 6.8 at the half switch, 3.4 in experiment 9, and 10.2, three steps, in the kernel before. What decides on one step or more stays open.

The wait at the half switch was 4.36 in the changed kernel's profile and between 2.59 and 4.38 in those of experiments 2 to 9, which leave that stage alone, so the loss there varies from run to run. In experiment 5 it was 3.17, with one step of half clock behind it instead of two.
